# A written order for the start, and two weight loads cut unevenly, in attention followed by a soft mixture of experts

## The chip, the cores and the metric

The kernel runs on one core of one Trainium2 chip. The metric is device time in microseconds. Its engines work in parallel, each through its own queue in order: PE (TensorE, matmuls), DVE (VectorE), ACT (ScalarE), POOL (GpSimd) and SP (SyncE). Transfers are issued by SP, ACT or POOL and are carried out by 16 DMA engines.

## The reference

Attention with 8 batches, 8 heads, 576 rows and 64 columns a head; a row sees 32 earlier rows, in heads 0 to 3 the nearest 32, in heads 4 to 7 every fourth of the last 128. Its output, 4608 rows of 512, is the input of a soft mixture of 8 experts with 4 slots each:

```python
scores = scale * np.matmul(q, k.transpose(0, 1, 3, 2))
attn = np.exp(np.where(masks, scores, -1e9) - max)   # then divided by its sum
x = (attn @ v)                                       # to [4608, 512]
logits = x @ phi                                     # [4608, 32]
d = softmax(logits, axis=0); slot_input = (d.T @ x).reshape(8, 4, 512)
slot_out[e] = np.maximum(slot_input[e] @ w1[e], 0.0) @ w2[e]
out = softmax(logits, axis=1) @ slot_out             # [4608, 512]
```

Inputs and output are float32 in HBM. w1 and w2 are 2 MB for each expert.

## The kernel before

**Loads.** POOL issues nearly all of them, and they change float32 to float16 on the way. Seven SBUF tiles `home0` to `home6` and later `home7` hold the raw q, k and v of one batch each (`load_batch`, L161 to L201), and then the weights of one expert each, w1 in columns 0 to 4095 and w2 in columns 4096 to 8191 (`load_w1` L237, `load_w2` L253). A row of w1 or w2 in a partition is 4096 numbers, 16 KB read and 8 KB written. The weights of experts 0 to 6 can only be loaded once the batch in that home is used up; `load_w2` takes experts 0 to 5 in one transfer of 128 partitions each, and the last two in parts, so that the left half of the output columns is complete before the right half. Up to eight of POOL's transfers are in flight: each waits for the landing of the eighth before it. The order of POOL's queue is written out by hand.

**Attention.** A unit is two heads of one batch, 32 units in all (`unit`, L275). `regroup` (L281) lays raw q and k of two plain heads side by side on VectorE; `transposes` (L292) brings q and k into columns on PE and copies them out; `scores` (L330) multiplies; `softmax_parts` (L362) takes the exponential on ScalarE and applies the masks on VectorE; `select_v` (L209) and `spread_v` (L204) bring v of one batch into the form for `values` (L422), which sums and divides. The first unit's q and k come on their own by SP and ACT (L89), ahead of POOL's queue. `warm` (L418) are matmuls without a use for the result, which start PE on data made by a memset.

**Experts and output.** `x_transposes` (L460), the logits and the slot sums follow unit by unit in the loop. After it come the experts: `expert_in` (w1, L712), `expert_turn` (L726, hTp L731), `expert_out` (w2, `sop`, L741). The left half of the columns is finished first: `so` (L796), then the products with the token weights (`f`, L782), scaled on ScalarE (L786) or VectorE (L788) and stored by SP (L791); then the right half.

**Order.** POOL's order and, after the loop, the order of PE, VectorE and ScalarE are as written (`tc.manual_schedule`). Ahead of the loop and in it a scheduler places the instructions of these three engines. PSUM tiles are shared: `ps_s` has two buffers, used by the scores (L341 to L352) and by the first two parts of `select_v` (L216); `ring` has two for the transposes, the third part of `select_v` (L227) and others. Ahead of the loop the kernel calls, in this order, `spread_constants`, `transposes(0)`, `spread_v(0)`, `transposes(1)`, `select_v(0)`, `scores(0)`, `softmax_parts(0, st)`, `regroup(2)` and `transposes(2)`; `spread_phi` (L585) comes in the loop at u == 1.

Of the kernel before, what the change touches and what calls it, by code (L numbers as in the profile page):

```python
# [37 lines left out]
OUT_COLS = [sum(nj for _, nj in OUT_TILES[:i]) for i in range(len(OUT_TILES))]  # L38
NU = 4 * B
NV = 2  # L40
SIDES = ((0, DMODEL // 2), (DMODEL // 2, DMODEL))
PIECES = ((0, 6), (6, 8))
HALF = 4
# [16 lines left out]
def kernel(  # L60
# [10 lines left out]
    nc = tc.nc  # L71
# [10 lines left out]
    heat = P1[:, 0].rearrange("p a t -> p (a t)")  # L82
# [4 lines left out]
    for n, (nm, ten, by) in enumerate((("qp", q, nc.sync), ("kp", k, nc.scalar))):  # L87
        first[nm] = stage[0:NP, 768 * n : 768 * n + 768].rearrange("p (g x) -> p g x", g=2)
        by.dma_start(  # L89
            out=first[nm],  # L90
            in_=ten[0, 0:2].rearrange("h s d -> (h s) d").rearrange("(g p r) d -> p g (r d)", g=2, r=RP),
# [112 lines left out]
    def spread_v(b):  # L204
        nc.vector.tensor_copy(
            out=vd[b % 2][:, :, 0:D], in_=raws[b]["vd"].rearrange("p h r d -> p (h r) d")
        )

    def select_v(b):  # L209
        raw, last = raws[b]["vp"], raws[b]["vt"]  # L210
        for i in range(2):
            sel = ps_s.tile([128, 2, 2, 4, D], FP32, name=f"sel{b}_{i}", tag="s")
            for r in range(4):
                for n in range(2):
                    rows = slice(64 * i + 32 * n, 64 * i + 32 * n + 32)
                    nc.tensor.matmul(  # L216
                        sel[:, n, 0],
                        pick[rows, r].rearrange("p i j -> p (i j)"),
                        raw[rows, :, r, :],
                        start=(r == 0),  # L220
                        stop=(r == 3),
                        tile_position=(64 * i + 32 * n, 0),
                    )
            nc.scalar.copy(out=vp[b % NV][:, 2 * i : 2 * i + 2, :, 0:D], in_=sel[:, :, 0])
        end = ring.tile([128, 2, 4, D], FP32, name=f"sel{b}_2", tag="ring")
        for r in range(4):
            nc.tensor.matmul(  # L227
                end.rearrange("p a h d -> p (a h) d"),
                pick[96:112, r].rearrange("p i j -> p (i j)"),
                last[:, :, r, :],  # L230
                start=(r == 0),
                stop=(r == 3),
                tile_position=(96, 0),
            )
        nc.scalar.copy(out=vp[b % NV][:, 4:6, :, 0:D], in_=end)

# [16 lines left out]
    def load_w2(e):  # L253
        w2t = w_tiles[e][1]
        w2_from = moe_w2[e].rearrange("(p c) f -> p c f", p=128)
        if e == E_EXP - 2:
            nc.gpsimd.dma_start(
                out=w2t[:, 0:HALF].rearrange("p c f -> p (c f)"),
                in_=w2_from[:, 0:HALF].rearrange("p c f -> p (c f)"),
            )  # L260
            load_half(e, 0)
            return
        if e < E_EXP - 2:
            nc.gpsimd.dma_start(
                out=w2t.rearrange("p c f -> p (c f)"), in_=w2_from.rearrange("p c f -> p (c f)")
            )
            return
        w2t = w_tiles[e][1] = w2t.rearrange("p c f -> p (c f)").rearrange("p (s c f) -> p s c f", s=2, c=8)
        for n, (d0, d1) in enumerate(SIDES):
            if n == 1:  # L270
                load_half(e - 1, 1)
            for c0, c1 in PIECES:
                nc.gpsimd.dma_start(out=w2t[:, n, c0:c1], in_=w2_from[:, c0:c1, d0:d1])
# [7 lines left out]
    def regroup(u):  # L281
        b, hp = unit(u)
        if hp >= 2:
            return
        for nm in ("q", "k"):
            t = side_by_side(nm, u)
            nc.vector.tensor_copy(
                out=t.rearrange("p r (h d) -> p r h d", h=2),
                in_=raws[b][nm + "p"][:, 2 * hp : 2 * hp + 2].rearrange("p h (r d) -> p r h d", d=D),
            )  # L290

    def transposes(u):  # L292
        b, hp = unit(u)
        for nm in ("q", "k"):
            if nm == "q":
                dst = qT_pool.tile([128, S], FP16, name=f"qT{u}", tag="qT")
                qTs[u] = dst
            else:
                dst = kTp if hp < 2 else kTd
                kTs[u] = dst  # L300
            if hp < 2:
                rg = ring.tile([128, RP, NP], FP16, name=f"rg{nm}{u}", tag="ring")
                for r in range(RP):
                    nc.tensor.transpose(rg[:, r, :], regrouped[nm, u][:, r], ident[0:NP, 0:NP])  # L304
                nc.scalar.copy(  # L305
                    out=dst[:, 0:S].rearrange("c (p r) -> c p r", r=RP),
                    in_=rg.rearrange("c r p -> c p r"),
                )
            else:
                raw = raws[b][nm + "d"]  # L310
                rg = ring.tile([128, 3, 4, ND], FP16, name=f"rg{nm}{u}", tag="ring")
                for a in range(3):
                    for cc in range(2):
                        j = 2 * a + cc
                        nc.tensor.transpose(  # L315
                            rg[:, a, 2 * cc : 2 * cc + 2, :].rearrange("c h p -> c (h p)"),
                            raw[:, hp - 2, 128 * j : 128 * j + 128],
                            ident[0:NP, 0:NP],
                        )
                (nc.scalar.copy if nm == "q" else nc.vector.tensor_copy)(  # L320
                    out=dst[:, 0:S].rearrange("c (g p a) -> c g p a", g=4, a=3),
                    in_=rg.rearrange("c a g p -> c g p a"),
                )
                if nm == "k":
                    nc.vector.tensor_copy(
                        out=ends[:, :, 1:65].rearrange("p h (t a e) -> p h a t e", a=2, e=2)[:, :, :, :, 0],
                        in_=dst[:, 0:S].rearrange("p (a h t) -> p h a t", a=2, h=2)[:, :, :, 128:CL],
                    )
# [89 lines left out]
    def warm(n, rhs, to=wps[:, 0]):  # L418
        for _ in range(n):
            nc.tensor.matmul(to[:, 0 : rhs.shape[1]], rhs[:, 0:128], rhs, start=True, stop=True)  # L420
# [159 lines left out]
    def spread_constants():  # L580
        nc.vector.reduce_sum(stackI, ident.rearrange("p (j s) -> p s j", j=4), axis=AX.X)
        for r in range(4):
            nc.vector.tensor_copy(out=pick[:, r, :, r], in_=stackI)

    def spread_phi():  # L585
        for kc in range(4):
            part = slice(32 * kc, 32 * kc + 32)
            nc.vector.tensor_copy(out=phi_by[part, kc], in_=phi_sb[part])
        pp = ring.tile([128, 4, N_SLOTS], FP32, name="pp", tag="ring")
        for r in range(4):  # L590
            nc.tensor.matmul(
                pp,
                pick[:, r].rearrange("p i j -> p (i j)"),
                phi_by[:, :, r, :],
                start=(r == 0),
                stop=(r == 3),
            )
        nc.vector.tensor_copy(out=phi4, in_=pp[:, :, None, :].broadcast_to([128, 4, 4, N_SLOTS]))

    warm(14, heat)  # L600
    ctx.enter_context(tc.manual_schedule(engines={mybir.EngineType.Pool}))
    for b in range(B):
        load_batch(b)
        if b == 0:
            nc.gpsimd.dma_start(out=phi_sb, in_=moe_phi.rearrange("(p r) s -> p r s", r=4))
    spread_constants()
    transposes(0)
    spread_v(0)
    transposes(1)
    select_v(0)  # L610
    st = scores(0)
    pr = softmax_parts(0, st)
    regroup(2)
    transposes(2)
    for u in range(NU - 2):
        st = scores(u + 1)
        if u + 3 < NU:
            regroup(u + 3)
        values(u)
        softmax_parts(u + 1, st)  # L620
        if u + 3 < NU:
            transposes(u + 3)
        b, ph = divmod(u - 4, 4)
        if b >= 0:
            if ph == 1:
                front_logits(b)
            elif ph == 2:
                front_rows(b)
            elif ph == 3:
                front_slots(b)  # L630
        if u == 1:
            spread_phi()
        if u >= 1:
            x_transposes(u - 1)
        if u % 4 == 3 and u // 4 + 1 < B:
            spread_v(u // 4 + 1)
            select_v(u // 4 + 1)
        if u % 4 == 2 and u // 4 < E_EXP - 1:
            load_w1(u // 4)
            if u // 4 < E_EXP - 3:  # L640
                load_w2(u // 4)
        if 26 <= u:
            nc.gpsimd.memset(hTp[u - 26], 0.0)
# [10 lines left out]
    st = scores(NU - 1)  # L654
# [20 lines left out]
    for c in range(2):  # L675
# [14 lines left out]
        out=siT,  # L690
# [144 lines left out]
```

## Time and profile before

| what | value |
|---|---|
| three runs, us | 181.28, 181.50, 181.54; median 181.5 |
| profiled execution, us | 181.12 |
| its span, us | 179.4 (179.36), granted PE clock 0.902 |
| PE, DVE, ACT, POOL busy, share of the span | 81%, 69%, 65%, 30% |
| read from HBM, written, MB | 62.02, 9.44 |

The span runs from the first to the last instruction; the profiled execution's time has 1.76 us more around it. A busy share is an average over stages that have different limits. The page has, in turn, the engines' busy time, the span in 40 slices, the DMA queues, the chain of work that ended last, and the costliest groups of instructions; the trace behind it has each instruction, each DMA packet with its start and length, and the 16 completions with which each transfer ends, one from each DMA engine. A packet's row names its queue and not its DMA engine.

### The profile page before, as it was taken

Reading aid. Unit: us, or ns where it says so; the run is one execution under the profiler, and the core shown is the slowest. Engines: PE = TensorE matmul, PEld = TensorE weight load, DVE = VectorE, ACT = ScalarE, POOL = GpSimd, SP = SyncE. Lnnn points to the kernel's source line nnn. Section 1 sums busy time; section 2 is a strip of 40 time slices with the busy share of each in tenths; the row PEclk is TensorE's granted clock in tenths of the full one; section 3 lists DMA queues with packets and bytes.
Section 4 is the critical chain, followed back from the end, with each engine's and each line's share of the span. In section 5 each row is a group of like instructions: output and inputs, shape, how many; then the busy total and the mean of one; then the engine's idle time right before and its main releaser. Section 6 shows DMA issues by size and latency. Waiting matters only on the chain.

```text
span 179.4 us, 5142 instructions
## 1 busy us (share of the span) xinstructions
PE 145.9 (81%) x2138; PEld 98.0 (55%) x2138; DVE 124.1 (69%) x341; ACT 116.2 (65%) x216; POOL 52.9 (30%) x86
## 2 busy tenths in 40 slices
PE   6549988999989989989998998998888997797000
PEld 2324666777576667667666757765658343342000
DVE  7407699689799978978979979876862011799200
ACT  2236768687888789789789788877721131699100
POOL 7946545454554644401110005006111100000000
PEclk9975699579999999999999999999998599999755
DMA  5999999999999999999999999999999999999995
GB/s 154 193 199 202 202 203 201 201 203 202 203 202 201 202 201 204 219 221 210 212 225 212 216 219 212 217 216 210 223 214 214 212 194 192 264 384 422 433 425 227
DMA packets 29238, 41.11 MB, mean 229 GB/s; under 512 B 1696, under 2 KB 26400, under 8 KB 26784
## 3 DMA queue, kind: packets, MB, share of 16 engines
q0 software_dynamic: 24416, 30.68, 98.0%
q1 hardware_dynamic: 4592, 9.82, 14.1%
q10 hardware_dynamic: 208, 0.29, 0.6%
q8 instruction: 16, 0.26, 0.5%
q14 instruction: 6, 0.05, 0.1%
HBM read 62.02 MB, written 9.44 MB: 398 GB/s over the span
## 4 chain that ended last, share of the span: by engine, by line
PE 30%; DMA 28%; DVE 17%; ACT 9%; issue 5%; POOL 3%; DVEq 0%; ACTq 0%; POOLq 0%
DMA home<-in_moe_w_dram 24%; PE o L448 6%; DMA home<-in_v_dram 4%; PE rgx L468 4%; ACT qT L305 4%; DVE ot L788 4%; PE sel L227 3%; PE l L486 3%; ACT pr L369 3%; PE s L343 3%; DVE x L453 3%; DVE P L395 2%; PE f L782 2%; DVE kTd L320 2%; PE u L549 2%
## 5 line engine op out<-in xcount | busy, mean ns | idle before, releaser
L453 DVE TENSOR_TENSOR x<-o,rc 128x640 f16<-128x640 f32 x32 | 26.3, 821 | 0.4
L369 ACT ACTIVATE pr<-s 128x960 f16<-128x960 f32 (+1 forms) x32 | 22.9, 761 | 1.6 <-PE s L343 1.6
L376 ACT ACTIVATE pd<-s 128x640 f16<-128x640 f32 x32 | 22.0, 713 | 2.1 <-PE s L352 2.0
L171 POOL DMA_DIRECT2D home<-in_v_dram x24 | 16.6, 692 | 14.9 <-DMA home<-in_k_dram 8.8
L448 PE MATMUL o<-vd,P 128*128 128x65 f16 x256 | 14.5, 198 | 3.2 <-DVE x L453 2.6
L240 POOL DMA_DIRECT2D home<-in_moe_w_dram x8 | 4.2, 531 | 40.8 <-PE rgq L315 33.4
L474 ACT COPY xT<-rgx 128x512 f16<-128x512 f16 x16 | 9.4, 586 | 10.2 <-PE rgx L468 10.2
L448 PEld LDWEIGHTS <-P 128*128 128x128 f16 x288 | 12.2, 100 | 6.8 <-DVE x L453 3.6
L385 DVE TENSOR_TENSOR Pp<-pr,fixed 128x1280 f16<-128x1280 f16 (+1 forms) x32 | 15.4, 497 | 0.3 <-ACT pr L369 0.3
L448 PE MATMUL o<-vp,Pp 128*128 128x65 f16 x288 | 15.3, 201 | 0.0
L468 PE MATMUL rgx<-fixed,x 128*128 128x128 f16 x155 | 14.0, 222 | 1.3 <-DVE x L453 0.6
L448 PEld LDWEIGHTS <-Pp 128*128 128x128 f16 x288 | 12.0, 102 | 4.1 <-issue 2.4
L788 DVE TENSOR_SCALAR ot<-f,rrow 128x256 f32<-128x256 f32 (+1 forms) x24 | 12.8, 610 | 2.1 <-PE f L782 2.1
L305 ACT COPY qT<-rgq 128x576 f16<-128x576 f16 x16 | 10.2, 639 | 6.1 <-PE rgq L304 5.4
L395 DVE TENSOR_TENSOR P<-pd,fixed 128x1024 f16<-128x1024 f16 x16 | 10.8, 672 | 4.7 <-ACT pd L376 4.7
L468 PEld LDWEIGHTS <-x 128*128 128x128 f16 x160 | 10.1, 98 | 6.6 <-issue 4.2
L786 ACT ACTIVATE ot<-f,rrow 128x256 f32<-128x256 f32 (+1 forms) x24 | 11.9, 601 | 2.5 <-PE f L782 1.7
L320 ACT COPY qT<-rgq 128x576 f16<-128x576 f16 x16 | 10.2, 640 | 4.1 <-PE rgq L315 4.0
L782 PE MATMUL f<-so,ET 128*128 128x256 f16 (+1 forms) x48 | 10.7, 324 | 2.3 <-ACT ot L786 1.1
L320 DVE COPY kTd<-rgk 128x576 f16<-128x576 f16 x16 | 12.3, 772 | 0.0
L197 POOL DMA_DIRECT2D home<-in_k_dram x15 | 10.0, 667 | 7.8 <-DMA home<-in_q_dram 7.1
L315 PEld LDWEIGHTS <-home 96*128 96x128 f16 x192 | 10.4, 103 | 3.3 <-DMA home<-in_q_dram 2.0
(119 smaller groups left out, 319.4 us busy)
## 6 DMA issues: line engine op xcount, KB each, us to landing
home<-in_moe_w_dram POOLq DMA_DIRECT2D x14, 1024.0 KB, 28.0
out_dram<-ot SPq DMA_DIRECT2D x5, 1024.0 KB, 7.8
home<-in_q_dram POOLq DMA_DIRECT2D x15, 288.0 KB, 9.8
home<-in_k_dram POOLq DMA_DIRECT2D x15, 288.0 KB, 9.9
home<-in_v_dram POOLq DMA_DIRECT2D x16, 256.0 KB, 9.8
out_dram<-ot SPq DMA_DIRECT2D x8, 256.0 KB, 2.9
out_dram<-ot SPq DMA_DIRECT2D x4, 512.0 KB, 7.2
home<-in_moe_w_dram POOLq DMA_DIRECT2D x2, 384.0 KB, 22.5
```

The lines of the kernel that those rows point to most:

```text
L171: nc.gpsimd.dma_start(out=dst, in_=v[b, h0 : h0 + n_h, r0 : r0 + 4 * n_p, :].rearrange("h (p r) d -> p h (r d)", r=4),)
L305: nc.scalar.copy(out=dst[:, 0:S].rearrange("c (p r) -> c p r", r=RP), in_=rg.rearrange("c r p -> c p r"),)
L320: (nc.scalar.copy if nm == "q" else nc.vector.tensor_copy)(out=dst[:, 0:S].rearrange("c (g p a) -> c g p a", g=4, a=3), in_=rg.rearrange(" ...
L369: nc.scalar.activation(out=(pr[:, :, 0 : 3 * QW], pr[:, :, 3 * QW :])[part], in_=st[:, :, 0 : (480, 224)[part]], func=AF.Exp, scale=SCALE,)
L376: nc.scalar.activation(out=pr[:, part].rearrange("p c e t -> p e c t"), in_=st[:, :, 0 : 2 * DW].rearrange("p e (c t) -> p e c t", c=2), f ...
L385: nc.vector.tensor_tensor(out=Pp[:, :, b0 : b0 + nb, 0:w], in0=pr[:, :, b0 * QW : b0 * QW + nb * w].rearrange("p h (t c) -> p h t c", c=w) ...
L395: nc.vector.tensor_tensor(out=P1.rearrange("p a c t -> p (a c) t"), in0=pr[:, :, :, 0:128].rearrange("p a c t -> p (a c) t"), in1=mask[:, ...
L448: nc.tensor.matmul(ot[:, h, blk], lhs, rhs, start=(n == 0), stop=(n == len(mms) - 1), skip_group_check=True)
L453: nc.vector.tensor_tensor(out=xs[b][:, :, 2 * D * hp : 2 * D * hp + 2 * D].rearrange("p t (h d) -> p h t d", h=2), in0=ot[:, :, :, 0:D], i ...
L468: nc.tensor.transpose(rg[:, 128 * blk : 128 * blk + 128], x[:, blk, hl : hl + 128], ident)
L782: nc.tensor.matmul(fp, ET[:, c0 : c0 + 127 * nj + 1 : nj], so[:, d0:d1], start=True, stop=True)
L788: nc.vector.tensor_scalar(out=ot[:, j], in0=fp, scalar1=scale, scalar2=None, op0=ALU.mult)
```

## The change

Two things. Ahead of the loop, PE, VectorE and ScalarE now follow the written order, in which the first unit's scores and softmax come straight behind its transposes; v, the second and third unit's transposes and `spread_phi`, which was in the loop, follow; two of the 14 warm matmuls stand behind the scores. In the built program the first unit's `values` stand on PE among the transposes of the second and third unit. And w2 of experts 1 and 4 is no longer loaded by one transfer of 128 partitions but by six: 112 partitions whole, then 3 partitions of 256 columns, 8 partitions whole, 8 partitions of 256 columns, 8 partitions of 3584 columns and 5 partitions of 256 columns.

```diff
+UNEVEN = (
+    (0, 112, 0, 4096), (125, 128, 0, 256), (112, 120, 0, 4096),
+    (120, 128, 256, 512), (120, 128, 512, 4096), (120, 125, 0, 256),
+)
...
         if e < E_EXP - 2:
-            nc.gpsimd.dma_start(
-                out=w2t.rearrange("p c f -> p (c f)"), in_=w2_from.rearrange("p c f -> p (c f)")
-            )
+            whole = w2t.rearrange("p c f -> p (c f)"), w2_from.rearrange("p c f -> p (c f)")
+            pieces = UNEVEN if e in (1, 4) else ((0, 128, 0, 4096),)
+            for p0, p1, x0, x1 in pieces:
+                to, of = (ap[p0:p1, x0:x1] for ap in whole)
+                nc.gpsimd.dma_start(out=to, in_=of)
             return
...
-    warm(14, heat)
+    warm(12, heat)
...
+    head = tc.manual_schedule(
+        engines={mybir.EngineType.PE, mybir.EngineType.DVE, mybir.EngineType.Activation}
+    )
+    head.__enter__()
     spread_constants()
     transposes(0)
+    pr = softmax_parts(0, scores(0))
+    warm(2, heat)
+    select_v(0)
+    regroup(2)
+    transposes(1)
+    transposes(2)
     spread_v(0)
-    transposes(1)
-    select_v(0)
-    st = scores(0)
-    pr = softmax_parts(0, st)
-    regroup(2)
-    transposes(2)
+    spread_phi()
+    head.__exit__(None, None, None)
     for u in range(NU - 2):
...
-        if u == 1:
-            spread_phi()
```

## The prediction

> **What bounds the kernel now.** I read the page's DMA queues first, then the chain of waits from 104 us on, then the timeline at both ends, and last the single packets and completions in the trace.
>
> ```profile
> q0 software_dynamic: 24416, 30.68, 98.0%
> q1 hardware_dynamic: 4592, 9.82, 14.1%
> q8 instruction: 16, 0.26, 0.5%
> ```
>
> GpSimd's queue q0 fills the 16 DMA engines; stores (q1) and instruction fetches (q8) share them. The chain in order of time:
>
> ```profile
> 107.80 27.18 DMA home<-in_moe_w_dram
> ...
> 140.13 15.06 DMA home<-in_moe_w_dram
> 155.19 0.04 issue
> 155.24 0.30 PE sop L741 x2
> ...
> 155.63 0.43 DVE so L796
> ```
>
> The last weight lands at 155.19. The timeline near it (start, busy time, engine, line) shows that the compute side is no earlier:
>
> ```profile
> 139.68 3.61 PE L712 MATMUL h<-home,siT 128*32 128x512 f16 x32 [0.38 <-DVE siT L689]
> ...
> 150.89 0.73 PE L741 MATMUL sop<-home,hTp 128*32 128x512 f16 x16 [0.27 <-DVE hTp L731]
> ...
> 151.66 0.37 ACT L796 CAST so<-sop 128x256 f16<-128x256 f32 x1 [3.65 <-PE sop L741]
> ...
> 153.08 3.30 SPq L791 DMA_DIRECT2D out_dram<-ot  x5
> ...
> 155.24 0.29 PE L741 MATMUL sop<-home,hTp 128*32 128x256 f16 x2 [0.28 <-DMA home<-in_moe_w_dram]
> ```
>
> The left half's last piece of w2 completes at 151.24 (completions in the trace) and the last matmuls on it start at 151.34, a start set by the PE run that began at 150.89 behind hTp. So the stores could begin only some 0.05 us earlier by compute alone.
>
> Each transfer ends with 16 completions, one for each engine, and those of the last w2 piece run from 152.32 to 155.19. Store packets first appear at 154.35. So most engines then stand idle, while the latest still has 0.55 us of load. The completions of one store are as far apart in the first (155.37 to 155.98) as in the last (177.63 to 178.20). The late engines carry that debt to the end: **the end is the latest engine's load plus 23 us of stores.**
>
> Where the debt comes from: at 18.2 us the lags run from 0 to 1.22 us. q8's 16 packets of 16 KB take 0.89 to 0.97 us each, one about every 8 us from 20.0 to 148.6. Their lengths repeat after eight (935, 974, 974, 961, 893, 893, 948, 945 ns, nearly the same again), and after each, one completion falls back by about 1.1 us. Followed from transfer to transfer, eight engines take two fetches each and end 2.03 to 2.91 us behind the first; the other eight take none and end 0, 0.01, 0.04, 0.30, 0.58, 0.87, 1.11 and 1.64 behind. The 1.64 had three of q14's 8 KB packets.
>
> **The change, part by part.** *Written order of the head.* The timeline before:
>
> ```profile
> 6.85 0.65 ACT L305 COPY kTp<-rgk 128x576 f16<-128x576 f16 x1
> ...
> 8.19 0.61 PE L216 MATMUL sel<-home,pick 32*128 32x256 f16 x13 [1.65 <-DMA home<-in_v_dram]
> ...
> 11.88 0.45 PEld L315 LDWEIGHTS <-home 96*128 96x128 f16 x6 [0.94 <-DMA home<-in_k_dram]
> ...
> 12.80 0.58 PE L343 MATMUL s<-qT,kTp 64*128 64x160 f16 x6
> ...
> 18.91 1.20 PE L448 MATMUL o<-vp,Pp 128*128 128x65 f16 x18
> ...
> 22.50 0.43 DVE L409 TENSOR_TENSOR P<-pd,fixed 128x128 f16<-128x128 f16 x1
> ```
>
> The operands of the first scores are ready at 7.50, but in PE's queue they stand behind sel and L315, which wait for v, q and k; they start at 12.80. Now they come first: scores 7.5 to 8.5, exp (0.97 + 0.55) to 9.7, masks (0.95) to 10.6. sel must wait for exp, since both s buffers are full, and follows at 9.1 and 9.7; the four L227 matmuls (1.88) to 12.1; values (1.20) with the L315 and L304 transposes between end near 16, against 20.1. That lead is not kept whole. VectorE's new order puts req of batch 1 ahead of ends; its q lands at 14.86. So ends is done at 15.5, the second unit's scores start near 16.0 (16.29 before), and vd 0.43, phi_by 1.10, rc 0.22, rek 0.36, x 0.82, phi 0.68, P 0.63 and 0.43, kTd 0.79, P 0.43 follow: L409 ends at 21.4 instead of 22.93. I take 1.5 us; between 0 (all lost at the waits on batch 1) and 4. The same 14 warm matmuls run, two later; no DMA issue of the head moves, on SP, ACT or POOL. From about 50 us on each engine's order is the old one, and a batch takes 14.5 us there, so the lead arrives at the end: h at 138.2 instead of 139.68. There the loads end last: the lead is worth the 0.05 us above. It is a cushion: compute could come later by 1.5 us and cost nothing.
>
> *Two w2 in six transfers.* All 16 engines move rows at one pace: a row of 16 KB read starts 606 ns after the one before, a 512 B packet 41 ns, a completion 21 ns. Until now each engine moves eight rows of a w2. Afterwards seven; rows 112 to 119 whole and 3584 of 4096 columns of rows 120 to 127 go out in two transfers of eight rows, the other 512 columns in transfers of 3, 8 and 5. No transfer of before has fewer than 16 rows, so which engines get these, and whether all 16 write a completion, is not in the trace. With the two big ones on the same eight engines, each such engine gets 530 ns (3584/4096 of 606) more and five completions (105): +0.635 us, twice +1.27. The others lose 606 and gain two small packets and five completions (187): -0.42, twice -0.84. If each engine writes completions only for its own rows, it is +1.15 and -0.96. On POOL ten more issues (L264 takes 0.53) are 5 us in a stretch where POOL waits for landings; with eight transfers in flight, each waits for the eighth before it, the w1 behind the first group until 85.2 while loads up to 95.7 are queued. The last ten issues wait as before.
>
> [...]
>
> **The cases.** *A, the extra rows fall on the eight engines without fetches (0.44).* Latest of these: 1.64 + 1.27 = 2.91; latest of the others 2.91 - 0.84 = 2.07. The latest engine was 2.91 behind and is so again: 0.00, or -0.12 with completions on own rows only; with 0.05 from the head **-0.1 us**. Own time: the profiled run took 181.12 us, span 179.36 and 1.76 around it, so 181.0. The median of the three runs shown (181.5) is 0.38 above it; some of that may be compute coming late, which the cushion would take, so I add little more than 0.3: **181.3**, in a range of its own of 180.9 to 181.6.
>
> *B, some of the eight carry fetches (0.27), slower.* From the first such engine on it decides: 2.03 + 1.27 = 3.30 to 2.91 + 1.27 = 4.18, against 2.91: +0.39 to +1.27, middle +0.8, so 182.2. For it: q0's first packets start one engine after another, some 57 ns apart, from 3.92 to 4.78. Followed from there, of the first two one carries fetches, the last two do and the one before them does not, so no eight neighbours in this order are all free. Against it: whether short transfers are dealt in that order is not seen.
>
> *C, faster by more than 0.36 us (0.26).* The end can go down to where no engine has load left when the stores begin, 0.55 us. It takes the engine at 1.64 being spared its two late q14 delays (0.51 and 0.50): then 1.1 + 1.27 = 2.4 decides and the whole 0.5 comes, 181.0 or, with the cushion in the median runs, 180.8. For it: those packets belong to engines whose streams change in the head; against: their number hardly changes.
>
> *D, each small transfer costs its own time on every engine (0.03).* Before, the 64 KB piece of v follows a 256 KB one at 0.35 to 0.45 us on the same engine, which is its packets' time; there is no gap. [...]
>
> A difference of 0.2% (0.36 us) is about what a measurement of this kernel can tell from no change. A gives 0.12 faster, 0.31 same, 0.01 slower; B and D slower; C faster. Faster 0.38, same 0.31, slower 0.31. The range takes in most of B and C: 180.7 to 182.4.
>
> **What would show it.** The first L343 (scores) starts at 7.5 to 8 instead of 12.80, L409 ends near 21.4, L712 starts near 138.2 and L741's run of 16 waits for a DMA. The completions of the last w2 piece: in A the latest stays near 2.9 us behind the first or moves under 2.6 in C; in B it is over 3.2. Wrong would be: h not earlier (then the head's waits ate it), a gap in q0 between 75 and 130 us (the eight in flight ran out), or an end that moves while the latest completion does not.

## The result, and the profile after

The changed kernel takes 182.05 us (median of 9 runs, 181.84 to 182.31) against 181.5 (9 runs, 181.05 to 182.0): the ratio is 1.003, interval 1.0016 to 1.0043, so it is slower by 0.3 to 0.8 us. Its profiled execution took 182.15 us with a span of 180.37; that of the kernel before took 181.12 with 179.36.

The DMA queues first, on the page of the changed kernel (queue, packets, MB, share of the 16 engines' span):

```profile
q0 software_dynamic: 24704, 30.68, 97.6%
q8 instruction: 16, 0.26, 0.5%
```

The bytes and the 16 instruction fetches are as before; q0 has 288 packets more. Now the chain of waits of the changed kernel at its end (start, us, what):

```profile
129.07 23.16 DMA home<-in_moe_w_dram
152.27 0.30 PE sop L751 x2
152.59 0.38 ACT so L806
...
155.54 0.76 PE sop L751 x9
156.30 0.41 PE sop L751 x2
156.80 0.44 DVE so L806
```

The end comes 1.0 to 1.2 us later: the last matmuls start at 156.30 instead of 155.24, `so` at 156.80 instead of 155.63. The chain now passes through the left half's last piece (landed at 152.23, 151.24 before) and PE's work behind it; the right half's last piece lands at 156.25 (155.19 before), again 0.05 us ahead of the last matmuls. Both pieces came later. The 16 completions of the last w2 piece tell how (us behind the first of them; the first and the last also from the span's start):

```
before  152.32  0 .05 .06 .32 .59 .86 1.14 1.65   2.07 2.28 2.39 2.45 2.50 2.59 2.65 2.88   155.19
after   151.65  0 .14  1.98 2.05 2.15 2.16 2.22 2.32 2.44 2.66 2.89 3.23 3.81  4.04 4.34 4.61   156.25
```

The first engine is done 0.67 us earlier, the last 1.06 later. Each of the two unevenly cut w2 does a part of it: 2.51 us from first to last completion in the transfer that completes from 88.5 us on, 3.05 at the end of the first group of six, 3.56 one w1 later, 4.17 at the end of the second group, 4.54 after the next w1. And the span is the last completion plus 24.12 us of output; before it was plus 24.17.

The compute side did what the written order is for. The timeline of the changed kernel at the start, and then from 137 us (start, busy time, engine, line; in brackets the idle time ahead and what ended it):

```profile
8.21 0.48 PE L349 MATMUL s<-qT,kTp 64*128 64x160 f16 x10 [1.02 <-ACT kTp L311]
...
20.84 0.42 DVE L415 TENSOR_TENSOR P<-pd,fixed 128x128 f16<-128x128 f16 x1
```

```profile
137.22 3.60 PE L722 MATMUL h<-home,siT 128*32 128x512 f16 x32 [0.38 <-DVE siT L699]
...
151.60 0.40 PE L751 MATMUL sop<-home,hTp 128*32 128x256 f16 x6 [1.70 <-DMA home<-in_moe_w_dram]
152.27 0.29 PE L751 MATMUL sop<-home,hTp 128*32 128x256 f16 x2 [0.27 <-DMA home<-in_moe_w_dram]
152.59 0.37 ACT L806 CAST so<-sop 128x256 f16<-128x256 f32 x1 [6.45 <-PE sop L751]
...
154.02 6.13 SPq L801 DMA_DIRECT2D out_dram<-ot  x8
```

The first scores run 4.6 us earlier (8.21 for 12.80), the first expert's h 2.46 us earlier (137.22 for 139.68). Then PE stands still for 1.70 us until a transfer lands at 151.56, and for 0.27 us more until the left half's last piece is complete, at 152.23 where it was 151.24. Whatever the head won is spent there, and the first stores leave 0.94 us later (154.02 for 153.08).

### The profile page after: what moved, and what is told of

Same layout as the page of the kernel before. It is cut to its first block, busy times and chain, and to the rows that moved or that the text cites. A ratio compares the mean times of both kernels' runs of the same rounds, so it can differ in the third digit from the quotient of the medians.

```text
span 180.4 us, 5159 instructions
## 1 busy us (share of the span) xinstructions
PE 147.0 (82%) x2138; PEld 98.7 (55%) x2138; DVE 124.7 (69%) x341; ACT 116.6 (65%) x216; POOL 58.2 (32%) x96
## 4 chain that ended last, share of the span: by engine, by line
PE 41%; DVE 22%; DMA 13%; ACT 12%; issue 4%; POOL 1%; DVEq 0%; ACTq 0%
DMA home<-in_moe_w_dram 13%; PE o L454 8%; ACT qT L311 5%; PE rgx L474 5%; PE sel L231 5%; DVE x L459 5%; ACT pr L375 4%; PE l L492 4%; DVE ot L798 4%; DVE P L401 3%; PE f L792 3%; PE s L349 3%; PE sel L220 3%; PE warm L426 3%; PE u L555 2%
## 5 line engine op out<-in xcount | busy, mean ns | idle before, releaser
L272 POOL DMA_DIRECT2D home<-in_moe_w_dram x16 | 8.3, 524 | 23.5 <-DMA home<-in_moe_w_dram 15.3
L311 ACT COPY qT<-rgq 128x576 f16<-128x576 f16 x16 | 10.2, 640 | 7.3 <-PE rgq L310 6.6
L792 PE MATMUL f<-so,ET 128*128 128x256 f16 (+1 forms) x48 | 11.2, 355 | 2.3 <-ACT ot L796 1.1
L244 POOL DMA_DIRECT2D home<-in_moe_w_dram x8 | 4.4, 548 | 22.2 <-DVE Er L529 4.7
L311 ACT COPY kTp<-rgk 128x576 f16<-128x576 f16 x16 | 10.3, 644 | 1.9 <-PE rgk L310 1.9
```

What stands on the lines that cost most here:

```text
L311: nc.scalar.copy(out=dst[:, 0:S].rearrange("c (p r) -> c p r", r=RP), in_=rg.rearrange("c r p -> c p r"),)
L792: nc.tensor.matmul(fp, ET[:, c0 : c0 + 127 * nj + 1 : nj], so[:, d0:d1], start=True, stop=True)
```

## The experiments

**Either part alone.** Theory: the six transfers are the whole loss and the head is worth nothing, as the loads end last. Rival: the head's order does the harm, or hides part of it. The first run has only the head's order, the second only the `UNEVEN` transfers.

> The written order of the head alone; w2 of experts 1 and 4 in one transfer each, as before. Theory (the DMA engine whose load ends last decides): no difference that can be measured, ratio 0.998 to 1.002, though L712 starts about 2.4 us earlier (137.2 against 139.68); the last w2 piece completes near 155.2 with the latest engine some 2.9 us behind the first. Rival (the head's order is what costs): ratio 1.003 as in the changed kernel.

> The six transfers alone, the head as before. Theory: ratio 1.003 or a little more (up to 1.006, since compute has no lead), the last w2 piece 4.0 to 4.7 us behind on the latest engine, complete near 156.2. Rival (the head costs): ratio 1.000.

Measured: head alone 181.64 us, ratio 0.9997, interval 0.9982 to 1.0012; transfers alone 182.06, ratio 1.0034, interval 1.0014 to 1.0053. With the head alone the last load lands at 155.58 and its completions are 3.16 us apart; with the transfers alone it lands at 156.22, with 4.96. The transfers are the whole of it. The 0.39 us between 155.19 and 155.58, without any change to the loads, show how much one profile differs from another. The timeline of the head alone:

```profile
137.63 3.34 PE L716 MATMUL h<-home,siT 128*32 128x512 f16 x32 [0.38 <-DVE siT L693]
...
150.90 1.05 PE L745 MATMUL sop<-home,hTp 128*32 128x256 f16 x8 [1.76 <-DMA home<-in_moe_w_dram]
```

h is early there too, and PE then waits 1.76 us for the load. Among nine profiled kernels without the head's order, h starts between 138.08 and 139.68 (mean 138.64). In the four with it (two of them follow below) it starts at 137.22, 137.63, 139.10 and 139.97 (mean 138.48). So 2.46 us flatters the lead, and by these profiles it doesn't reliably arrive at all.

**Short transfers by themselves.** A profile of the kernel before with 19 tiny extra loads of 2, 3 and 5 rows, whose packets can be told by their sizes, and a timed run with six transfers in the same two w2, each of a multiple of 16 partitions:

```diff
+UNEVEN = (
+    (0, 112, 0, 4096), (112, 128, 0, 256), (112, 128, 256, 512),
+    (112, 128, 512, 768), (112, 128, 768, 1024), (112, 128, 1024, 4096),
+)
```

> The kernel before with 19 tiny extra loads of 2, 3 or 5 partitions into a tile that nothing reads, each of its own width, so that the packets tell which DMA engine, counted in the order in which short transfers are dealt, is which in the trace. Theory: the eight engines with instruction fetches do not lie side by side in that order; of the engines 3 to 10 three or more carry fetches. Rival (dealing does not matter; every small transfer costs all engines alike): the engines 3 to 10 are free of fetches.

> The kernel before, w2 of experts 1 and 4 again in six transfers, but all six with a multiple of 16 partitions (112 rows, then 16 rows cut by columns into 256, 256, 256, 256 and 3072), so that every engine gets the same. Theory: every engine pays five completions and five more packets, about 0.12 us a time, 0.25 us in all; the latest engine stays 2.9 us behind the first; ratio 1.000 to 1.002. Rival (cutting into six is what costs): ratio 1.003 or more.

The six even transfers: 181.68 us, ratio 1.0017, interval 1.0001 to 1.0032; the last load lands at 155.52, 0.33 later than before, and the completions stay 3.0 us apart. So ten more transfers cost 0.2 to 0.3 us by themselves (the interval is 0.02 to 0.6), nothing near the 0.35 us each that a 64 KB piece of v took before (D). The interval overlaps that of the change (0.3 to 0.8), so the times alone do not tell the two apart; the spread of the completions does, 3.0 us here and 4.61 there. The run with the tiny loads (181.13 us) showed something else: all fifteen loads of two rows ran on the same two engines, and each load of five on the same five. The engines 3 to 10 of the expectation come from an assumption of the author's, that each short transfer begins where the one before ended; in these loads the start did not move, so what was expected of them could not be tested.

**No turning: 8 and 8.** If each short transfer began where the one before ended, 3, 8, 8, 8 and 5 (32 in all) would bring the start back to its place. If every one begins at the same engine, the transfers of 3 and 5 partitions turn nothing and can be left out.

```diff
+UNEVEN = ((0, 112, 0, 4096), (112, 120, 0, 4096), (120, 128, 0, 4096))
```

> The kernel before with the last 16 partitions of the same two w2 in two plain transfers of eight partitions each, with no transfers of 3 and 5 around them. Theory (a transfer of fewer than 16 rows always begins at the same engine, so the order 3, 8, 8, 8, 5 turns nothing): both fall on the same eight engines again, each gains 0.606 us of row and two completions of 0.021 per w2, twice +1.30 us, the other eight lose twice 0.56 us; the last load lands near 156.2 (155.19 before, 156.25 with the change), the completions of the last piece are 4.4 to 5.4 us apart, ratio 1.002 to 1.006. Rival (each short transfer begins where the one before ended): the first falls on eight engines and the second on the other eight, every engine has its eight rows again, the spread stays near 2.9 us, the last load lands near 155.3, ratio 0.999 to 1.002.

Measured: 182.14 us, ratio 1.0046, interval 1.0027 to 1.0064; last load at 156.72, completions 5.01 us apart. With a start that moves on, every engine would have had its eight rows and nothing would have changed. That rival is out.

**The map.** 19 loads again, one of each number of rows, and four into other partitions.

```diff
+PROBES = tuple((0, n) for n in range(1, 16)) + ((125, 3), (8, 8), (120, 8), (3, 10))
```

> The kernel before with 19 additional loads of a few bytes into an unused buffer (they change nothing that is computed): one each of 1 to 15 rows from partition 0 on, then 3 rows into partitions 125 to 127, 8 into 8 to 15, 8 into 120 to 127 and 10 into 3 to 12. Theory (always the same first engine): the packets of the load of n rows lie on nested sets of engines, each load adds one engine to the set of the load before it, and the last four lie on the sets of 3, 8, 8 and 10. Rival 1 (each begins where the last ended): successive loads lie on different engines. Rival 2 (the engine follows the partition): the last four lie on other engines than the loads of 3, 8 and 10 rows from partition 0. Time 181.1 to 181.8 by all three.

The start of each packet (us, from the trace; within a load in order of time):

```
3 rows          83.697 83.892 83.938
4 rows          83.725 83.921 83.966 84.664
6 rows          88.525 88.649 88.844 88.890 89.458 89.588
7 rows          93.421 93.544 93.739 93.785 94.237 94.353 94.483
8 to 8..15     117.628 118.030 118.371 118.417 118.493 119.092 119.723 120.049
8 to 120..127  117.659 118.062 118.403 118.449 118.525 119.124 119.755 120.080
```

How it is read: one load queued behind another on the same engine starts some 29 ns later, and the next w1 or w2 puts 4.896 us between two loads. 83.697, 83.892 and 83.938 return as 83.725, 83.921 and 83.966, so the load of four uses the engines of the load of three and one more (84.664). The load of seven has the six of 88.525 to 89.588, each 4.895 or 4.896 later, and a new one (94.237). So it goes on to 15 rows. The partition plays no part: the loads into 8 to 15 and 120 to 127 run on the same eight engines, 30 to 33 ns apart. A load of n rows lies on the first n engines of one fixed order, and rivals 1 and 2 are both out. This run took 182.34 us, over what was expected: the last piece's first completion is 0.57 us later than before. Why is not shown; in the run before it, with as many tiny loads, it was 0.11 us.

Followed through the same trace, two of the first eight engines carry instruction fetches (q8): the sixth falls back by 1.09 us at the fetch of 111.0, the seventh by 1.03 at that of 118.8. The first three, the fifth and the eighth do not fall back so. The fourth takes no fetch either, but two 8 KB packets of q14, the other instruction queue, at 78.0 and 128.9 us; the first set it back by 0.53 us.

**Which engine it is.** 13 and 3 partitions give a second row of these 16 to the first three engines only, 12 and 4 to the first four; the last three engines get none of the 16 in the one, the last four in the other. So the fourth engine is the only one with more to load in the second kernel than in the first (minus: the first kernel, plus: the second; both against the kernel before).

```diff
-UNEVEN = ((0, 112, 0, 4096), (112, 125, 0, 4096), (125, 128, 0, 4096))
+UNEVEN = ((0, 112, 0, 4096), (112, 124, 0, 4096), (124, 128, 0, 4096))
```

> The kernel before with the last 16 partitions of the same two w2 in transfers of 13 and 3 partitions. By the map, the first 13 engines take a row of the one and the first three a row of the other, so only the first three gain (0.606 us of row and 0.04 of completions per w2, twice +1.29 us). In the map run those three took no fetch and stood 0.72 to 0.84 us behind the first engine at 113 us, so they end about 2.1 us behind. Theory (only extra rows on an engine with fetches cost time): the latest engine is untouched but for 0.08 us of completions, the last load lands at 155.2 to 155.5, spread 2.7 to 3.1 us, ratio 0.999 to 1.002. Rival (full rows dealt unevenly cost time on whichever engines they fall, or short transfers of full rows do): as in the two transfers of eight, the last load near 156.3, ratio 1.003 to 1.006.

> As the run with 13 and 3 partitions, but with 12 and 4: one engine more, the fourth, gains two rows. In the map run the fourth took a fetch of about 1.05 us between 78.8 and 83.7 us. Theory: it is one of those that end 2.03 to 2.91 us behind, and with +1.29 it ends 3.3 to 4.2 behind; the last load lands 0.4 to 1.3 us later than before, at 155.6 to 156.5, one single completion far behind the others, ratio 1.001 to 1.006. Rival (which engine it is plays no part; the number of moved rows does): the same as with 13 and 3 within 0.3 us of the last landing.

The chain of the first, then of the second:

```profile
140.21 15.09 DMA home<-in_moe_w_dram
155.29 0.04 issue
155.34 0.30 PE sop L744 x2
```

```profile
126.65 25.24 DMA home<-in_moe_w_dram
...
156.46 0.44 DVE so L799
```

With three engines the last load lands at 155.29 (155.19 before) and the time is 181.63 us, ratio 1.0016, interval 0.9997 to 1.0034. With four it lands at 155.92, `so` starts at 156.46, and the time is 181.86, ratio 1.0034, interval 1.0018 to 1.0051. The completions of the last piece:

```
13 and 3  151.55  0 .90 1.07 1.33 2.15 2.23 2.23 2.29 2.45 2.89 3.15 3.20 3.23 3.25 3.48 3.75   155.29
12 and 4  151.99  0 .37 .46 .64 1.70 1.82 1.88 2.05 2.54 2.60 2.84 2.85 2.90 2.94 3.00  3.92   155.92
```

In the second, one single completion stands 0.92 us behind the other fifteen. The packets of its engine can be followed back by their times, as a row starts 606 ns after the one before: it has a second row in both w2, so it is one of the first four. It took no fetch, against what was expected. The eight fetches from 78.5 to 137.4 us run on eight other engines, none of them among the first four. It was set back by two q14 packets, at 77.6 and 128.1 us, as the fourth engine was in the map run; the fetch of that run which the expectation gives to the fourth (78.7 us) ran on another engine. The second of the two, among the rows of its engine:

```
queue, start us, ns   q0 127.493 625   q14 128.098 322   q0 128.417 894   q0 129.283 625
```

The row behind it starts 0.32 us later than without it and takes longer, 0.58 us in all. This engine stood 1.7 us behind the first at 85 us, ahead of both cut w2; two second rows added 1.29 and the packet 0.58. So the engine matters, as the theory says, but it is not a fetch that made it late. The intervals of the two times overlap; the landing and the lone completion, in one profile of each, are what tells them apart. The spread of the first (3.75) was expected at 2.7 to 3.1: forgotten was that three engines have a row less, so the first completion comes earlier while the last stays.

**Twice the amount.** The six transfers in four w2.

```diff
-            pieces = UNEVEN if e in (1, 4) else ((0, 128, 0, 4096),)
+            pieces = UNEVEN if e in (1, 2, 3, 4) else ((0, 128, 0, 4096),)
```

> The kernel before with the six transfers of 3, 8, 8, 8 and 5 partitions in four w2 instead of two. Theory (each of these w2 puts 0.635 us more on the same eight engines, three of which carry instruction fetches too): twice the cost of two such w2, which moved the last load by 1.06 us: the last load lands near 157.3, the spread of the last piece is 5.8 to 6.6 us, ratio 1.006 to 1.012. Rival (the cost is a fixed part of each added transfer, on every engine): the spread stays at most 4.6 us and all engines come later by about as much; with two such w2 in 16 partitions each the time rose by 0.2 us, so here by 0.4, ratio 1.001 to 1.004.

Measured: 183.77 us, ratio 1.0135, interval 1.0103 to 1.0167. The chain:

```profile
130.10 23.52 DMA home<-in_moe_w_dram
...
158.25 0.43 DVE so L802
```

The last load lands at 157.70, 2.51 us after that of before, for a sum of 4 x 0.635 = 2.54. The completions fall into groups: eight engines at 0 to 2.46 us, five at 3.94 to 5.19, three at 6.08 to 6.51. These are the eight with fewer rows, five of those with more rows, and the three of these that were late already. In the run with 8 and 8 the three latest (4.03, 4.22 and 5.01 us) can be followed: the first is the engine of the q14 packet of 128.6, the other two took the fetches of 109.9 and 118.0. The time grew by more than twice that of the change, and by more than the 1.006 to 1.012 expected, about as the landing did; the interval's lower end is still above what was expected of the rival.

**A version that uses the map.** If extra load costs nothing on the first three engines, the others can be relieved: one w2 in eight transfers, the last six of them of 3 or 2 rows, together with the head's order.

```diff
+UNEVEN = (
+    (0, 112, 0, 4096), (112, 128, 0, 1792), (112, 115, 1792, 4096), (115, 118, 1792, 4096),
+    (118, 121, 1792, 4096), (121, 124, 1792, 4096), (124, 126, 1792, 4096), (126, 128, 1792, 4096),
+)
...
+            pieces = UNEVEN if e == 4 else ((0, 128, 0, 4096),)
```

> The written order of the head, and one w2 (the second of the two) in eight transfers: 112 rows; 1792 columns of the last 16 rows; their other 2304 columns in 3, 3, 3, 3, 2 and 2 rows. By the map the first two engines take six of the short pieces, the third four, all others none. Each of the other 13 loses 0.5625 of a row, 0.34 us, and gains seven completions, 0.15 us: -0.19 us for the engines with fetches; the first two gain 5 x 0.34 + 0.15 = 1.86 us, to 2.6 or 2.7 behind the first engine, less than the latest with fetches. Theory: the last load lands 0.1 to 0.2 us earlier than in the kernel before (near 155.0 to 155.1 in a profile), ratio 0.997 to 1.000, a gain too small for a measurement to tell. Rival (the first two engines end latest): spread over 3.1 us, last load 155.4 to 156.2, ratio 1.001 to 1.004.

It took 185.73 us, ratio 1.0246, interval 1.0227 to 1.0264: far outside both. POOL's timeline and the busy times in stretches of 6 us (the last two columns are the DMA engines' share and GB/s):

```profile
101.24 0.51 POOL L272 DMA_DIRECT2D home<-in_moe_w_dram  x1 [4.23 <-DMA home<-in_moe_w_dram]
106.16 0.51 POOL L272 DMA_DIRECT2D home<-in_moe_w_dram  x1 [4.41 <-DMA home<-in_moe_w_dram]
...
120.71 0.51 POOL L272 DMA_DIRECT2D home<-in_moe_w_dram  x1 [4.37 <-DMA home<-in_moe_w_dram]
```

```profile
114.00:120.00 6.00, 5.54 (x88) 3.58 (x86) 4.78 (x14) 4.53 (x8) 0.50 (x1) 1.00 1.04 217
120.00:126.00 6.00, 5.35 (x82) 3.65 (x80) 4.35 (x12) 4.50 (x10) 0.99 (x2) 1.00 0.55 111
126.00:132.00 6.00, 4.30 (x84) 3.35 (x82) 4.80 (x11) 2.83 (x7) 6.00 (x12) 0.95 0.93 158
```

Up to eight of POOL's transfers are in flight, and with each landing of an old one, some 4.9 us apart, POOL could issue one more: a short piece each time. From 120.7 us on, all eight in flight were the pieces of this one w2, seven of them short. The next w1 could only be issued once the 112 rows had landed (124.95; it was issued at 125.5), and the pieces were all through by 126.1. In the second fence the DMA share falls from 1.04 to 0.55 and the rate from 217 to 111 GB/s: for some 4 us most engines had nothing to load. In the changed kernel whole loads are always among the eight, and the DMA share stays at 1.01 or more in every 6 us from 100 to 136.

The last run sends four pieces at once, two behind the next w1 and two behind the one after it:

```diff
-            for p0, p1, x0, x1 in pieces:
-                to, of = (ap[p0:p1, x0:x1] for ap in whole)
-                nc.gpsimd.dma_start(out=to, in_=of)
+            late.extend((whole, piece) for piece in pieces)
+            some_pieces(4)
...
         w_tiles[e] = [w1t, t[:, 4096:8192].rearrange("p (c f) -> p c f", c=8)]
+        some_pieces(2)
```

> The run with one w2 in eight transfers again, but only four of them go out at once; two follow the next w1 and two the w1 after that, so that eight transfers in flight never are all short ones of one w2. Theory (the 4 us gap in the loads of that run came from the eight in flight being nearly empty; the map stands): no gap, q0 busy to its end, the 13 engines with less to load 0.19 us earlier, the first two engines 2.6 to 2.7 us behind the first; the last load lands at 154.9 to 155.2, ratio 0.997 to 1.000, which a measurement can hardly tell from no change. Rival (short pieces cost more than their bytes wherever they stand): ratio above 1.003.

181.29 us against 181.58 for the kernel before, ratio 0.9988, interval 0.9971 to 1.0006: the gap is gone, as expected. Whether it is a gain stays open. The median is 0.3 us lower, but the interval holds 1, and in the profiled execution the last load landed at 155.75 instead of 154.9 to 155.2; there the completions were already 3.65 us apart at 101.7 us, before the unevenly cut w2, and 3.72 at the end. h started at 139.97 there in spite of the head's order. `x` (L453 of the kernel before) of the fourth unit still came early, at 27.27 us (29.97 in the kernel before, 28.19 in the changed one), that of the eighth no longer, at 45.72 (45.40 and 43.16). In between, from 36 to 42 us, TensorE was granted 0.54 of its clock, 1.00 in the changed kernel; that this is the whole reason is not shown.

## Why the prediction was wrong

**What bounds the kernel: right.** In all 13 profiled kernels the span is the last load's completion plus 24.1 to 24.2 us (24.4 with the six transfers in four w2), from 155.19 + 24.17 to 159.58 + 24.12.

**The head: right at the start and in its worth, not in the lead at the end.** The first scores started at 8.21 for 7.5 to 8 forecast, L409 (L415 now) ended at 21.26 for 21.4, and in the changed kernel PE then waits for a DMA. But the prediction let the 1.5 us arrive whole because each engine's order is the old one from 50 us on; of the four profiles with the head, two start h about 1.2 us ahead of the mean of the nine without, two 0.5 and 1.3 us behind it. Alone the head is worth nothing (0.9997), and it hides nothing either: the change has 1.003 with it, 1.0034 without.

**The sum of the rows: right.** It had +1.27 us for the engines with extra rows; the landing moved by 1.06 with two such w2 and by 2.51 (2.54 summed) with four. Two terms of it were the author's assumption: one set of eight engines for both big pieces, and 16 completions for each short transfer. The runs showed both afterwards: two loads of eight rows on the same eight engines in the map run, and 160 completions more on q0 in the changed kernel (1408, 1248 before), 16 for each of the ten more transfers.

**The step that failed is the likeliest case itself: "the extra rows fall on the eight engines without fetches".** Nothing in the trace of before spoke for it; the prediction had even written down, for B, that no eight neighbours in the order of the first packets are all free. The runs show that a transfer of fewer than 16 rows took the first engines of one fixed order (37 loads in two runs), and that the sixth and the seventh of them carried fetches (1.09 and 1.03 us in the map run). So case B happened, by its own mechanism: it had +0.39 to +1.27 us at the landing and 182.2 us; measured are +1.06 and 182.05. Of the three latest engines two carry fetches. The third, the fourth of the order, carries none, and by the times of its q14 packets (78.9 and 129.3 us before) it is the one that the prediction had at 1.64. A gave it no room: 1.64 + 1.27 is just the 2.91 of the latest, and with 12 and 4 rows it ended 0.92 us behind all others, in an execution in which it stood further back from the start (1.7 us at 85 us, some 1.1 before). So A's sum was too tight as well. The chances were the error. With half of the engines laden and the set unknown, a blind draw of eight misses all laden ones once in 12,870; A at 0.44 would have needed a row of the trace that tied the short transfers to the free engines.

**The transfers of 3 and 5 partitions turn nothing.** In the map run loads of 2 to 15 rows all began at one engine, and two transfers of eight cost 1.0046, where a start that moves on would have cost nothing. With 3, 8, 8, 8 and 5 the two big pieces fall on one set of eight whether the start moves on or not, which is why the sum held. A set turned by three, the fourth to the eleventh engine of the map, would have had the sixth and the seventh in it as well, so a start that moves on from the map's first engine would not have saved case A.

**C and D did not happen.** The last load did not come earlier (C). Ten more transfers of 16 partitions each and more cost 0.3 us in all, not ten times 0.35 (D).

**One of the signs named ahead was wrong.** The prediction would have read a spread over 3.2 us as case B. But engines that lose rows finish earlier, so the spread grows even where the end stays: with 13 and 3 partitions it was 3.75 us with the last load at 155.29. The sign to read is the last completion's own time.

**What stays open.** The profiles put the change's cost at 1.03 us, the medians at 0.55 (0.3 to 0.8). The lags differ from one execution to the next (completions 2.88 us apart in the profile of before, 3.16 with the head alone, 3.65 already at 101.7 us in the last run), and one profile of each kernel doesn't tell how they are distributed.

## What to carry to other kernels

Here 16 DMA engines shared each load and the end was the latest engine's (the last completion plus 24.1 to 24.4 us in all 13 profiles), so it mattered which engine got an extra row and how late that engine already was (last load at 155.29 with 13 and 3 rows, at 155.92 with 12 and 4), not only how many rows were moved: tiny loads with sizes of their own showed the engines in a single profile. Which packets made an engine late has to be followed packet by packet; a lag of the expected size was not proof of a fetch here. A transfer of fewer than 16 rows put them on the same first engines every time here (37 loads in two runs); a cut along the columns with rows in multiples of 16 kept the engines even (completions 3.0 us apart, 2.9 before). The limit of eight transfers in flight counted transfers here, not bytes: seven short ones in a row left the engines short of work behind them (DMA share 0.55 from 120 to 126 us).

## What the runs showed of the hardware

- GpSimd's loads of 2 to 15 rows ran on the first engines of one fixed order, whatever was loaded before them and whichever partitions they wrote (two runs, 37 such loads).
- Two more rows on one more engine, the fourth of that order, moved the last load from 155.29 to 155.92 us; with such rows on the first three engines it landed 0.1 later than before. These are single profiles; without any change to the loads it landed at 155.19 and 155.58.
- The eight instruction fetches of 16 KB from 78.5 to 137.4 us ran on eight engines, one each, and none on the first four of that order; an 8 KB packet of q14 (322 ns) set the fourth back by 0.53 to 0.58 us.
- One long and seven short pieces of one w2 in a row, with at most eight transfers in flight, took the DMA share from 1.04 to 0.55 for 6 us; that kernel took 4.4 us longer (185.73, 181.31 before).
